# Moving the landmarks' softmax between the two halves of C v

## The chip, the cores and the metric

The kernel runs on one NeuronCore of a Trainium2 chip. The metric is the device time of one execution in microseconds (us). Every engine of the core works through its own queue of instructions in order: TensorE (PE, with its weight loads shown as PEld), VectorE (DVE), ScalarE (ACT), GpSimd (POOL), and SyncE (SP), which here only issues transfers. Engines meet through semaphores.

## The reference, cut to what matters

Three stages follow each other: a Nystrom attention over 8 batches with 8 heads, 576 positions and head dimension 64, a squared-ReLU layer pair over the 4608 tokens (512 to 2048 to 512), and a top-1 mixture of 8 experts. The change is in the attention:

```python
q_lm = q.reshape(B, H, m, S // m, D).mean(axis=3)      # m = 32 landmarks
k_lm = k.reshape(B, H, m, S // m, D).mean(axis=3)
A = sm(q, k_lm)        # sm: scaled scores, softmax over the last axis
Bm = sm(q_lm, k_lm)
C = sm(q_lm, k)
Z = Bm.transpose(0, 1, 3, 2) / (norm1(Bm) * norm_inf(Bm) + 1e-06)
for _ in range(6):
    Z = 2 * Z - Z @ Bm @ Z
out = A @ Z @ C @ v
```

`Bm` is the landmarks' own softmax, 32 by 32 for each head. `C v` is 32 by 64 for each head. Both must be there before the iteration for `Z` starts.

## The kernel before

For each batch the attention is a "unit" of small steps (`unit`). Heads go in two groups of four (`hg` 0 and 1), with four heads times 32 landmarks on the 128 partitions. Batch 0's unit runs in a prologue of its own, with `u["early"]` set and with high priority. The units of batches 1 to 7 are side work: they are generated one step at a time, by `point`, while the main work of an earlier batch runs. The main work is `gemm`, with `second`: each batch in two halves of 288 columns, each half in 16 pieces of 6 matmuls into `hp` (line 998) and 12 into `acc` (line 1048). A rate for each half (`RATES`) says how many side steps come with each point. `weave` takes two lists of steps in turn. So the order in which instructions are written down is set by these rates and weaves; a scheduler at build time then orders each engine's queue by that order and by what its model holds to be ready, and gives out buffers.

What the change touches is in these functions:

- `scores_c` makes the scores of C for one head group and one half of the columns, copies them to `ec` (ACT), takes the maximum (DVE, line 497), and after the second half makes the exponential with the row sum in `mc[..., 3]` (ACT, line 504).
- `softmax_b` is the landmarks' own softmax, three steps: 16 small matmuls into a bank (line 346, input `lm`), maximum and exponential (lines 523 to 528), then a chain of small DVE instructions (lines 533 to 560) to the norms, and `diagonal` (line 647), which lays `Bm` out as the weights `dg` of the iteration. Two of its instructions, lines 557 and 560, have nothing to do with `Bm`: they turn the row sum of C into its reciprocal, `mc[..., 5]`.
- `transposed_c(u, j)`, j = 0, 1, 2, transposes four blocks of `ec` on PE (line 349, input `ec`) and copies them to `et` on ACT (line 572).
- `values(u, hg)` multiplies `et` by `v` for one head group on PE (line 346, inputs `v,et`, 24 products that show as 48 matmuls). It scales the result into `bc` on DVE (line 587). At its end it issues a load of `v`: `values(u, 0)` issues the three transfers of this batch's second half, `values(u, 1)` those of the next batch's first half (`load_v`, line 371, on SP). Each half has one buffer, so a load waits for the product that last read the buffer.
- `inverse` is the iteration (line 346, inputs `bc,dg` and then `eu,dg`).

PSUM banks of the side work come from one pool of three (`aux`, through `bank()`), which the main work also uses for the gate's logits and routing. `values(u, 0)` takes a bank for both halves of C v (`u["pc"]`) and it is free again when `values(u, 1)` has been scaled. During batch 1's unit (and until about 141 us) the first layer's weights of the second matmul are still being converted (`convert`: lines 153 to 167 and 191 on ACT, DVE and POOL).

Of the kernel before, what the change touches and what calls it, by code (L numbers as in the profile page):

```python
# [9 lines left out]
F32 = mybir.dt.float32  # L10
# [4 lines left out]
ALU = mybir.AluOpType  # L15
# [4 lines left out]
B, H, S, D = 8, 8, 576, 64  # L20
LM = 32
# [62 lines left out]
class Kernel:  # L84
# [395 lines left out]
    def scores_c(self, u, hg, c):  # L480

        nc = self.nc
        if hg == c == 0:
            u["mc"] = self.sm.tile([128, 2, 8], F32, tag="mc", name="mc")
            u["ec"] = self.wk.tile([128, 2, S], F32, tag="ec", name="ec")
        sc = self.bank()
        for h in range(4):
            p, x = self.columns(u, "k", hg, h, c)
            self.matmul(sc[32 * h:32 * h + 32, 0:HC], lhsT=u["ql"][p, hg, h, :], rhs=x, start=True, stop=True)
        to, src = u["ec"][:, hg], sc[:, 0:HC]  # L490
        if u["pe"]:
            to = to.rearrange("p (r c i l) -> p c i r l", c=2, i=3, l=LM)[:, c]
            src = src.rearrange("p (i r l) -> p i r l", i=3, l=LM)
        else:
            to = to[:, c * HC:(c + 1) * HC]
        nc.scalar.copy(out=to, in_=src)
        nc.vector.tensor_reduce(out=u["mc"][:, hg, c:c + 1], in_=sc[:, 0:HC], axis=AX.X, op=ALU.max)
        if c == 1:

            mc, ec = u["mc"][:, hg], u["ec"][:, hg]  # L500
            nc.vector.tensor_scalar(
                out=mc[:, 2:3], in0=mc[:, 0:1], scalar1=mc[:, 1:2], scalar2=-SCALE / SEG, op0=ALU.max, op1=ALU.mult
            )
            nc.scalar.activation(
                out=ec, in_=ec, func=ACTF.Exp, bias=mc[:, 2:3], scale=SCALE / SEG, accum_out=mc[:, 3:4]
            )

    def softmax_b(self, u):

        nc, sm = self.nc, self.sm  # L510
        wide = [128, 2, LM]
        pb = self.bank()
        for hg in range(2):
            for h in range(4):
                self.matmul(
                    pb[32 * h:32 * h + 32, 32 * hg:32 * hg + 32],
                    lhsT=u["ql"][0:64, hg, h, :], rhs=u["kl"][0:64, hg, h, :], start=True, stop=True,
                )
        pb = pb[:, 0:2 * LM].rearrange("p (g l) -> p g l", g=2)
        bc = u["bc"] = sm.tile([128, 2, LM + D], F32, tag="bc", name="bc")  # L520
        mb = u["mb"] = sm.tile([128, 2, 12], F32, tag="mb", name="mb")
        bm = bc[:, :, 0:LM]
        nc.vector.tensor_reduce(out=mb[:, :, 0], in_=pb, axis=AX.X, op=ALU.max)
        nc.vector.tensor_scalar(
            out=mb[:, :, 1], in0=mb[:, :, 0], scalar1=-SCALE / SEG / SEG, scalar2=None, op0=ALU.mult
        )
        for hg in range(2):
            nc.scalar.activation(
                out=bc[:, hg, 0:LM], in_=pb[:, hg], func=ACTF.Exp, bias=mb[:, hg, 1:2], scale=SCALE / SEG / SEG,
                accum_out=mb[:, hg, 2:3],  # L530
            )
        yield STEP
        nc.vector.tensor_scalar(out=mb[:, :, 2], in0=mb[:, :, 2], scalar1=1e-9, scalar2=None, op0=ALU.add)
        nc.vector.reciprocal(out=mb[:, :, 3], in_=mb[:, :, 2])
        nc.vector.tensor_tensor(out=bm, in0=bm, in1=mb[:, :, 3].unsqueeze(2).to_broadcast(wide), op=ALU.mult)
        bt = sm.tile([128, 3, 2, LM], F32, tag="bt", name="bt", bufs=1)
        for hg in range(2):
            nc.vector.transpose(out=bt[:, 0, hg], in_=bc[:, hg, 0:LM])
        nc.vector.tensor_reduce(out=mb[:, :, 4], in_=bm, axis=AX.X, op=ALU.add)
        nc.vector.tensor_reduce(out=mb[:, :, 5], in_=bt[:, 0], axis=AX.X, op=ALU.add)  # L540
        yield STEP
        nc.vector.tensor_copy(
            out=bt[:, 1:3].rearrange("p a g l -> p g a l"),
            in_=mb[:, :, 4:6].unsqueeze(3).to_broadcast([128, 2, 2, LM]),
        )
        bn = sm.tile([128, 2, 2, LM], F32, tag="qs", name="bn", bufs=1)
        nc.vector.transpose(
            out=bn.rearrange("p a g l -> p (a g l)"), in_=bt[:, 1:3].rearrange("p a g l -> p (a g l)")
        )
        nc.vector.tensor_reduce(  # L550
            out=mb[:, :, 6:8].rearrange("p g a -> p a g"), in_=bn, axis=AX.X, op=ALU.max
        )
        nc.vector.tensor_tensor(out=mb[:, :, 8], in0=mb[:, :, 6], in1=mb[:, :, 7], op=ALU.mult)
        nc.vector.tensor_scalar(out=mb[:, :, 8], in0=mb[:, :, 8], scalar1=1e-6, scalar2=None, op0=ALU.add)
        nc.vector.reciprocal(out=mb[:, :, 9], in_=mb[:, :, 8])
        nc.vector.tensor_scalar(out=mb[:, :, 10], in0=mb[:, :, 9], scalar1=-1.0, scalar2=None, op0=ALU.mult)
        nc.vector.tensor_scalar(
            out=u["mc"][:, :, 4], in0=u["mc"][:, :, 3], scalar1=1e-9, scalar2=None, op0=ALU.add
        )
        nc.vector.reciprocal(out=u["mc"][:, :, 5], in_=u["mc"][:, :, 4])  # L560
        self.diagonal(u, bc)
        yield STEP

# [10 lines left out]
    def values(self, u, hg):  # L574

        if hg == 0:
            u["pc"] = self.bank()
        b = u["b"]
        for r in range(R6):
            for h in range(4):  # L580
                self.matmul(
                    u["pc"][32 * h:32 * h + 32, hg * D:(hg + 1) * D],
                    lhsT=u["et"][:, R6 * hg + r, 32 * h:32 * h + 32],
                    rhs=self.vt[b, hg][:, h, r * D:(r + 1) * D],
                    start=(r == 0), stop=(r == R6 - 1),
                )
        self.nc.vector.tensor_scalar(
            out=u["bc"][:, hg, LM:], in0=u["pc"][:, hg * D:(hg + 1) * D], scalar1=u["mc"][:, hg, 5:6], scalar2=None,
            op0=ALU.mult,
        )  # L590
        if (b, 1) not in self.vt:
            self.load_v(b, 1)
        elif hg == 1:
            self.load_v(b + 1, 0)
# [84 lines left out]
    def unit(self, u):  # L679
# [23 lines left out]
                yield STEP  # L703

        def cv():
            yield from self.softmax_b(u)
            for j in range(2):
                self.transposed_c(u, j)
                yield STEP
            self.values(u, 0)  # L710
            yield STEP
            self.transposed_c(u, 2)
            yield STEP

# [29 lines left out]
        if u["early"]:  # L744
            yield from weave(self.sooner(itertools.chain(cv(), zcv())), itertools.chain(tq(), a()))
        else:
            yield from weave(cv(), tq())
            yield from weave(zcv(), a())
# [749 lines left out]
```

## Time and profile before

| | |
|---|---|
| Time, median of 3 runs | 1337.75 us (1334.39 to 1339.83) |
| Profiled execution | 1340.34 us, of which its span is 1338.5 us |
| PE busy | 1275.7 us, 95% |
| DVE busy | 781.5 us, 58% |
| ACT busy | 633.6 us, 47% |
| POOL busy | 384.5 us, 29% |
| Mean granted TensorE clock | 0.977 of full speed |

Busy times are of one profiled execution, the only one with a trace. The page cuts the span into 40 slices of 33.5 us; a digit is the busy share of a slice in tenths. A busy PE is not PE at its peak: the ends of matmuls are modelled. An engine's idle time is put down to the last event that released it.

### The profile page before, as it was taken

How to read it: one execution, taken by the hardware profiler on the slowest of the kernel's cores; microseconds unless marked ns; L12 is line 12 of the kernel's file. 1: busy time of each engine (PE TensorE's matmuls, PEld its weight loads, DVE VectorE, ACT ScalarE, POOL GpSimd, SP SyncE). 2: the span in 40 equal slices, each digit the busy share in tenths (PEclk: the TensorE clock that was granted, in tenths of full speed). 3: DMA queues.
4: the chain of work that ended last, by engine and by line, in shares of the span. 5: the costliest groups of instructions: out<-in, count | busy, mean ns of one | idle time of the engine just before them, and what ended most of it. 6: DMA issues, size and time to landing. Idle time of an engine off the chain costs nothing.

```text
span 1338.5 us, 25101 instructions
## 1 busy us (share of the span) xinstructions
PE 1275.7 (95%) x9458; PEld 1114.2 (83%) x9458; DVE 781.5 (58%) x1743; ACT 633.6 (47%) x1402; POOL 384.5 (29%) x311
## 2 busy tenths in 40 slices
PE   6587999999999999999999999999999999999997
PEld 4276868688788888898989999998888888888886
DVE  7999868768769897687653433454423233233231
ACT  5596454445535557545654344344334334334331
POOL 3566112113013034313622112024323323233120
PEclk7588999999999999999999999999999999999999
DMA  9866283462623247613652112014344354342321
GB/s 324 273 222 192 86 269 85 173 199 89 217 70 112 72 127 211 172 63 95 206 146 67 43 35 67 1 48 146 99 130 139 100 156 120 109 150 92 116 93 38
DMA packets 126587, 172.38 MB, mean 129 GB/s; under 512 B 10558, under 2 KB 84062, under 8 KB 126462
## 3 DMA queue, kind: packets, MB, share of 16 engines
q1 hardware_dynamic: 126030, 170.11, 41.6%
q8 instruction: 76, 1.25, 0.4%
q0 software_dynamic: 288, 0.43, 0.1%
q14 instruction: 49, 0.40, 0.1%
q10 hardware_dynamic: 144, 0.20, 0.0%
HBM read 128.19 MB, written 42.51 MB: 128 GB/s over the span
## 4 chain that ended last, share of the span: by engine, by line
PE 74%; DVE 11%; DMA 7%; ACT 3%; issue 2%; POOL 1%; SPq 1%; POOLq 0%; DVEq 0%; ACTq 0%
PE acc L1048 24%; PE hp L1238 15%; PE y L1274 13%; PE hp L998 11%; PE bank L346 6%; PE y L1286 2%; DMA raw<-in_moe_w_in_dram 2%; DVE sums L382 2%; DVE gl L1015 2%; DMA g<-gs 2%; DVE g L1011 1%; PE pl L1075 1%; DVE m L164 1%; DMA w<-win 1%; DMA t<-in_q_dram 1%
## 5 line engine op out<-in xcount | busy, mean ns | idle before, releaser
L1048 PE MATMUL acc<-gh,wo 128*128 128x288 f32 x2048 | 459.2, 300 | 1.6 <-POOL wo L191 0.7
L1048 PEld LDWEIGHTS acc<-gh,wo 128*128 128x128 f32 x2048 | 344.1, 190 | 27.1 <-issue 18.2
L1048 PE MATMUL acc<-gl,wo 128*128 128x288 f32 x1024 | 290.3, 301 | 10.2 <-DVE gl L1015 9.7
L998 PE MATMUL hp<-ab,gb 128*128 128x288 f32 x1536 | 254.8, 301 | 0.9 <-ACT r L1009 0.5
L998 PEld LDWEIGHTS hp<-ab,gb 128*128 128x128 f32 x1536 | 217.7, 189 | 19.6 <-issue 6.9
L1011 DVE TENSOR_TENSOR g<-r 128x288 f32<-128x288 f32 x239 | 130.3, 546 | 162.5 <-ACT r L1009 161.7
L1009 ACT ACTIVATE r<-hp 128x288 f32<-128x288 f32 x256 | 105.8, 413 | 245.1 <-PE hp L998 240.6
L1238 PEld LDWEIGHTS hp<-xs,s 128*128 128x128 f32 x1536 | 210.7, 188 | 9.0 <-issue 0.9
L1238 PE MATMUL hp<-xs,s 128*128 128x288 f32 x1536 | 215.5, 295 | 0.0
L1048 PEld LDWEIGHTS acc<-gl,wo 128*128 128x128 f32 x1024 | 194.6, 190 | 22.8 <-DVE gl L1015 17.5
L1274 PE MATMUL y<-s,h 128*128 128x512 f32 x768 | 190.3, 395 | 0.0
L1274 PEld LDWEIGHTS y<-s,h 128*128 128x128 f32 x768 | 141.0, 188 | 29.4
L1015 DVE TENSOR_TENSOR gl<-g,gh 128x288 fp32r<-128x288 f32 x256 | 143.2, 560 | 26.8 <-ACT gh L1014 8.9
L191 POOL TENSOR_TENSOR s<-r,s 128x512 fp32r<-128x512 f32 x64 | 83.1, 1299 | 245.6 <-ACT s L188 245.6
L191 DVE TENSOR_TENSOR s<-r,s 128x512 fp32r<-128x512 f32 x64 | 53.1, 830 | 154.4 <-ACT s L188 154.4
L191 POOL TENSOR_TENSOR gb<-gr,gb 128x512 fp32r<-128x512 f32 x56 | 74.5, 1331 | 226.6 <-ACT gb L188 143.6
L188 ACT CAST s<-r 128x512 fp32r<-128x512 f32 x128 | 78.2, 616 | 118.8 <-PE y L1286 92.6
L1247 DVE SCALAR_TENSOR_TENSOR h<-hp,h 128x64 fp32r<-128x64 f32 (+2 forms) x192 | 62.6, 354 | 109.5 <-ACT h L1244 109.5
L1014 ACT ACTIVATE gh<-r 128x288 fp32r<-128x288 f32 x256 | 114.4, 447 | 6.4
L1244 ACT ACTIVATE h<-hp 128x288 fp32r<-128x288 f32 x128 | 52.6, 411 | 132.1 <-PE hp L1238 118.2
L382 DVE TENSOR_REDUCE sums<-t 128x32 f32<-128x576 f32 x64 | 71.2, 1165 | 9.3 <-DMA t<-in_q_dram 5.8
L191 POOL TENSOR_TENSOR xs<-xr,xs 128x1152 fp32r<-128x1152 f32 x16 | 45.7, 2860 | 68.3 <-ACT xs L188 63.2
(195 smaller groups left out, 1350.8 us busy)
## 6 DMA issues: line engine op xcount, KB each, us to landing
r<-in_moe_w_dram SPq DMA_DIRECT2D x128, 256.0 KB
w<-win SPq DMA_DIRECT2D x80, 256.0 KB
gr<-g SPq DMA_DIRECT2D x56, 256.0 KB
t<-in_k_dram SPq DMA_DIRECT2D x16, 576.0 KB
t<-in_q_dram SPq DMA_DIRECT2D x16, 576.0 KB
v<-in_v_dram SPq DMA_DIRECT2D x48, 192.0 KB
x_d<-x SPq DMA_DIRECT2D x16, 576.0 KB
xr<-x_d SPq DMA_DIRECT2D x16, 576.0 KB
```

The source lines that it names most:

```text
L188: hi = self.nc.scalar.copy(out=t[:, 0], in_=raw)
L191: (lo_eng or self.nc.gpsimd).tensor_tensor(out=t[:, 1], in0=raw, in1=t[:, 0].bitcast(F32), op=ALU.subtract)
L346: self.last_pe = self.nc.tensor.matmul(out, **kw)
L382: self.nc.vector.tensor_reduce(out=s[:, 0, ds], in_=t[:, :, ds].rearrange("p s d -> p d s"), axis=AX.X, op=ALU.add)
L998: mm = nc.tensor.matmul(hp[:, 0:HC], lhsT=g[:, l, hg, fs], rhs=at[:, r, hg, :], start=(i == 0), stop=(i == 5))
L1009: nc.scalar.activation(out=r, in_=hp[:, 0:HC], func=ACTF.Relu, scale=1.0 / 256)
L1011: nc.vector.tensor_tensor(out=g2, in0=r, in1=r, op=ALU.mult)
L1014: nc.scalar.activation(out=gh, in_=r, func=ACTF.Square)
L1015: nc.vector.tensor_tensor(out=gl, in0=g2, in1=gh.bitcast(F32), op=ALU.subtract)
L1048: nc.tensor.matmul(acc[m][:, 0:HC], lhsT=self.wo[f][:, l, ms], rhs=r, start=(f == 0 and i == 0), stop=(f == NFC - 1 and i == 2),)
L1238: nc.tensor.matmul(hp[:, 0:HC], lhsT=s1[:, l, kk, :], rhs=xs[j, c][:, r, kk, :], start=(k == 0), stop=(k == 3 * KD - 1),)
L1274: mm = nc.tensor.matmul(acc[t], lhsT=l, rhs=s2[:, r, :], start=(first and k == 0), stop=(last and k == 2))
```

## The change

For batches with `u["early"]` unset, that is 1 to 7, the three steps of `softmax_b` are made after `values(u, 0)` and not ahead of `transposed_c(u, 0)`. So that `values(u, 0)` has what it needs, the two instructions for the reciprocal of C's row sum move to the end of `scores_c`, for batch 0 too, and the tile `bc`, which both write parts of, is made by whichever comes first.

```diff
@@ scores_c
+        if hg == c == 1:
+            mc = u["mc"]
+            nc.vector.tensor_scalar(out=mc[:, :, 4], in0=mc[:, :, 3], scalar1=1e-9, scalar2=None, op0=ALU.add)
+            nc.vector.reciprocal(out=mc[:, :, 5], in_=mc[:, :, 4])
+
+    def place_bc(self, u):
+        if "bc" not in u:
+            u["bc"] = self.sm.tile([128, 2, LM + D], F32, tag="bc", name="bc")
+        return u["bc"]
@@ softmax_b
-        bc = u["bc"] = sm.tile([128, 2, LM + D], F32, tag="bc", name="bc")
+        bc = self.place_bc(u)
...
-        nc.vector.tensor_scalar(
-            out=u["mc"][:, :, 4], in0=u["mc"][:, :, 3], scalar1=1e-9, scalar2=None, op0=ALU.add
-        )
-        nc.vector.reciprocal(out=u["mc"][:, :, 5], in_=u["mc"][:, :, 4])
@@ values
-            out=u["bc"][:, hg, LM:], in0=u["pc"][:, hg * D:(hg + 1) * D], scalar1=u["mc"][:, hg, 5:6], scalar2=None,
+            out=self.place_bc(u)[:, hg, LM:], in0=u["pc"][:, hg * D:(hg + 1) * D], scalar1=u["mc"][:, hg, 5:6], scalar2=None,
@@ unit
         def cv():
-            yield from self.softmax_b(u)
+
+            if u["early"]:
+                yield from self.softmax_b(u)
             for j in range(2):
                 self.transposed_c(u, j)
                 yield STEP
             self.values(u, 0)
             yield STEP
+            if not u["early"]:
+                yield from self.softmax_b(u)
             self.transposed_c(u, 2)
             yield STEP
```

## Rows read from the trace of the kernel before

**Rows 1.** The page, section 1, and PE in 40 slices.
```profile
PE 1275.7 (95%) x9458; PEld 1114.2 (83%) x9458; DVE 781.5 (58%) x1743; ACT 633.6 (47%) x1402; POOL 384.5 (29%) x311
...
PE   6587999999999999999999999999999999999997
```

**Rows 2.** Stretches: length, busy us (instructions) by engine, PE clock, DMA share, GB/s.
```profile
60.00:140.00 80.00, 66.82 (x538) 54.55 (x535) 75.01 (x125) 62.55 (x151) 48.91 (x37) 0.91 0.62 195
140.00:660.00 520.00, 506.87 (x4311) 433.65 (x4310) 405.25 (x921) 274.10 (x640) 136.71 (x127) 1.00 0.46 140
660.00:1330.00 670.00, 666.96 (x4261) 605.81 (x4259) 249.38 (x578) 264.46 (x545) 172.15 (x117) 1.00 0.33 97
```

**Rows 3.** Waits of PE from 60 us on: us in total, times, longest us.
```profile
PE acc L1048 <- DVE gl L1015: 9.7, 11, 2.8
PE bank L346 <- DMA v<-in_v_dram: 3.4, 2, 2.1
PE bank L346 <- ACT et L572: 1.6, 1, 1.6
...
PE bank L346 <- DVE bc L587: 1.0, 1, 1.0
...
PE bank L346 <- ACT gs L934: 0.8, 2, 0.6
```

**Rows 4.** PE in order of time, 100 to 130 us: start, us, line, operation.
```profile
109.57 1.51 PE L346 MATMUL bank<-v,et 96*32 96x64 f32 x48
...
117.11 0.43 PE L346 MATMUL bank<-v,et 96*32 96x64 f32 x16 [2.13 <-DMA v<-in_v_dram]
```

**Rows 5.** PE in order of time, 186 to 219 us (batch 2's unit).
```profile
195.91 0.43 PE L346 MATMUL bank<-v,et 96*32 96x64 f32 x16 [1.64 <-ACT et L572]
...
202.23 0.46 PE L346 MATMUL bank<-bc,dg 128*128 128x96 f32 x2 [1.04 <-DVE bc L587]
...
207.21 0.88 PE L346 MATMUL bank<-v,et 96*32 96x64 f32 x48 [1.30 <-DMA v<-in_v_dram]
...
213.12 0.58 PE L346 MATMUL bank<-eu,dg 128*128 128x96 f32 x4
...
218.07 0.58 PE L346 MATMUL bank<-eu,dg 128*128 128x96 f32 x4
```

**Rows 6.** SP's issues in order of time, 106 to 215 us.
```profile
111.14 1.28 SPq L371 DMA_DIRECT2D v<-in_v_dram  x3
...
197.03 1.86 SPq L371 DMA_DIRECT2D v<-in_v_dram  x3
```

**Rows 7.** Short stretches, columns as in rows 2.
```profile
118.75:122.15 3.40, 3.40 (x47) 2.95 (x49) 3.37 (x5) 2.75 (x6) 1.32 (x2) 0.50 0.00 0
197.25:200.65 3.40, 3.11 (x14) 2.77 (x13) 2.20 (x4) 1.14 (x3) 0.81 (x1) 0.50 1.03 317
```

**Rows 8.** DVE in order of time, 92 to 130 us.
```profile
111.15 0.28 DVE L587 TENSOR_SCALAR bc<-bank,mc 128x64 f32<-128x64 f32 x1 [0.22 <-PE bank L346]
...
118.42 2.28 DVE L382 TENSOR_REDUCE sums<-t 128x32 f32<-128x576 f32 x2 [0.91 <-DMA t<-in_q_dram]
```

**Rows 9.** Groups by line, DVE, 60 to 660 us: busy, mean ns, idle before.
```profile
L647 DVE TENSOR_TENSOR dg<-bc,h 128x256 f32<-128x256 f32 x7 | 4.0, 573 | 0.0
...
L523 DVE TENSOR_REDUCE mb<-bank 128x2 f32<-128x64 f32 x7 | 1.4, 203 | 0.0
```

**Rows 10.** DVE in order of time, 16 to 34 us (batch 0's unit).
```profile
23.90 0.17 DVE L557 TENSOR_SCALAR mc<-mc 128x2 f32<-128x2 f32 x1
...
28.24 0.24 DVE L587 TENSOR_SCALAR bc<-bank,mc 128x64 f32<-128x64 f32 x1
```

**Rows 11.** PE in order of time, 436 to 456 us (batch 5's unit).
```profile
437.99 0.29 PE L346 MATMUL bank<-lm 64*32 64x32 f32 x12
...
438.98 0.60 PE L349 MATMUL bank<-ident,ec 128*96 128x128 f32 x4
```

**Rows 12.** Waits of SP's queue, whole span.
```profile
SPq L371 <- PE bank L346: 32.1, 12, 7.9
```

## The prediction, made blind

> **What bounds the kernel now.** I read the page first, then stretches, then the waits of the engine that they point to, and then single instructions around the changed code. The page says that PE is busy for 95% of the span, and its row of slices is a line of nines after the first 130 us [rows 1]. The stretches say where the rest is: in 60 to 140 us PE is busy 66.82 of 80 us, and DVE 75.01 of 80, so that stretch is paced by DVE, which still converts weights there. From 140 to 660 us PE is idle for 520.00 - 506.87 = 13.1 us, from 660 to 1330 us for only 3.0 us [rows 2]. The units of batches 1 to 7 run between 60 and 660 us. So nearly everything that the change touches is side work beside an engine that is already full, and it counts only as far as PE stands still for it, or as far as a standstill lowers PE's clock.
>
> The waits of PE name the standstills [rows 3]. The largest, 9.7 us in 11, is main work: `acc` waits for `gl` from a late DVE. Next come 3.4 us in 2 for the load of `v`, 1.6 us for a copy of `et`, 1.0 us for `bc`. All of these touch the code that is moved, so the question is which of them the new order takes away and which it makes.
>
> **The two waits for v.** In batch 1, `values(u, 0)` starts at 109.57 us, takes 1.51, and `values(u, 1)` is held until 117.11 us with 2.13 us of idle before it [rows 4]. In batch 2 the first half's last products run at 195.91 us and the second half is held until 207.21, with 1.30 us idle [rows 5]. The loads are issued as soon as the first half has read the buffer: at 111.14 us and at 197.03 us [rows 6]. From the first issue to the end of the wait is 117.11 - 111.14 = 6.0 us and 207.21 - 197.03 = 10.2 us. The load cannot start before the product that empties its one buffer, so only a longer way from the first half to the second hides it.
>
> **What the change does to that way.** `cv` and `tq` are woven, one step of each in turn. Before, 4 steps lie between `values(u, 0)` and `values(u, 1)` in batches 2 to 7: a step of `tq`, `transposed_c(u, 2)`, two more of `tq`. After, the three steps of `softmax_b`, with three of `tq` between them, come on top: 10 steps. For batch 1, with fewer steps in `tq`, it is 2 and then 8. What a step lasts is read from the iteration, which is also woven one to one: 218.07 - 213.12 = 4.95 us for two steps, some 2.5 us each [rows 5]. Six more steps are an estimated 15 us. As the scheduler may pull side work together, I count on half of it, and 7 us still cover the 1.30 and the 2.13 us. So both waits go, in the order as written.
>
> **What they are worth.** In batch 2 PE is the bound, and the gain is the 1.30 us. For batch 1 the ends are further apart. After the wait of 2.13 us the granted clock is 0.50, or 1.2 GHz in place of 2.4, from 118.75 to 122.15 us, and PE is busy all 3.40 us of it [rows 7]; at full clock that work would take 1.70 us. So the upper end is 2.13 + 1.70 = 3.8 us. The lower end is set by DVE, which in this stretch has no time to give: around the wait it idles only 0.22 and 0.91 us [rows 8], 1.1 us in all. What PE wins above that, it would lose again at the next `gl`. I take 1.7 us, near the lower end, since DVE was the busier of the two [rows 2]. Together 3.0 us.
>
> The Trainium skill (DMA: Bandwidth & Descriptors, "Anatomy of one DMA") gives a transfer about 2.0 us plus its bytes over 436 GB/s, fitted on GpSimd's path. By that the 590 KB of one half would be there an estimated 3.4 us after the issue, no half would be waited for, and the change would hide nothing: 0 in place of 3.0 us. The 6.0 and 10.2 us of this trace [rows 4, 5, 6] differ from it, and go.
>
> **The moved steps themselves.** Nothing is added or dropped. For one batch `softmax_b` with `diagonal` is 16 small matmuls, 2 exponentials, and 19 DVE instructions between 203 ns (the first, line 523) and 573 ns (the last, line 647) [rows 9], by the means of the same view 4.8 us of DVE. They come later, by six steps. Who needs them next is `inverse(u, 0)`, and from the end of `softmax_b` to it there are still a step of `tq`, `transposed_c(u, 2)`, two of `tq`, `values(u, 1)` and one of scores: six steps, by the same 2.5 us some 15 us against 4.8 us of work. That cover is why I cost the move at nothing. Were it gone, `inverse` would wait as it does once for `bc`, 1.0 us [rows 3], in up to 7 batches: 0 to 7 us. The count of steps for a unit stays, so a unit ends where it did, and no batch's main work is held longer.
>
> The pair for the reciprocal (lines 557 and 560) goes from `softmax_b` to `scores_c`. In batch 0 it runs at 23.90 us, and its reader at 28.24 [rows 10]: over 4 us of room, so the prologue stays. In the others it could stand in DVE's queue and wait for the exponential; behind it would be the main work's `gl`. The scheduler put it after the exponential already; I cost it at 0, with 1 us for one late `gl` (9.7 / 11 is 0.9 us) [rows 3] as the upper end.
>
> Transfers: the three issues of `values(u, 0)` come earlier. SP stands before such an issue until PE has read the buffer, 32.1 us in 12, 2.7 us each [rows 12], and loads of `g` queue behind it. That stays as it is, only earlier; its longest, 7.9 us, was covered by loaded `g`, since no wait of PE names them [rows 3]. Cost 0.
>
> **Sum.** 1.30 + 1.7 = 3.0 us off. The profiled execution took 1340.34 us (span 1338.5 and 1.8 around it), which gives 1337.3; it lies 2.6 us above the median of the runs, so against the median the forecast is 1337.75 - 3.0 = 1334.8 us. About 0.5%, 6.7 us, is what a measurement of this kernel can tell from no change; this is less.
>
> **Rivals.**
>
> *More goes than the waits for v* (1328 us). In batch 2 the copies of `et` and of `bc` made PE wait 1.64 and 1.04 us [rows 5], the former followed by 197.25 to 200.65 us at clock 0.50 [rows 7]: another 1.7 us. If the new order takes these along with the full 3.8 us of batch 1, it is 1.30 + 3.8 + 1.64 + 1.04 + 1.7 = 9.5 us. For it: all lie in the moved stretch. Against it: DVE paces batch 1, and the `et` wait may only change places.
>
> *Nothing comes out* (1337.8 us). The scheduler may lay down nearly the same order, or the 1.30 us is eaten by one new wait. For it: in batch 5 the transposes of C run 1.0 us after the landmark products [rows 11], though the text puts two more steps of each list between them; so the executed order is not the written one.
>
> *Slower: C v loses its cover* (1345 us). `softmax_b` stood between the exponential of C and its transposes. Now `transposed_c` follows `scores_c` at once, and PE's queue is in order: if a transpose or a product reaches PE before the exponential or the copy of `et` is done, main work behind it waits too. The price by the one such wait is 1.64 us, and with a stretch at half clock 3.3 us. It shows as slower from (6.7 + 3.0) / 3.3, three batches of seven, on; at three it is 1334.8 + 9.9 = 1345. Against it: two woven steps still lie between the last scores and the blocks of the second head group, and the scheduler waits for what its model knows.
>
> *Slower: banks* (1342 us). The bank of C v is now held for 10 steps, and two of three are left for landmark products, transposes, the pieces of `g` and the gate. One wait of PE for a bank's reader (`gs`) is 0.4 us [rows 3], with half clock 2.1; in half of the batches 7 us. Against it: the pool is used little at a time by batches 3 to 5. The Trainium skill (Perfetto Trace Analysis, "Identifying the Most-Contended Engine" and what follows it) reads a gap that repeats on the saturated engine as a possible lack of PSUM; the trace before shows no such repeating gap.
>
> **Chances.** Forecast 0.48 (its own range 1331.5 to 1338), nothing comes out 0.14, more goes 0.24, lost cover 0.09, banks 0.05. Faster by over 0.5% is the case in which more goes, 0.24; slower the last two together, 0.14; within 0.5% the rest, 0.62. The range reaches to the cases on both sides, 1327 to 1344 us: it leaves out the far half of each.
>
> **What would show it.** In the profile after, PE's wait for `v` [rows 3] should be gone, with at least 10 us between the two halves of C v in each of batches 1 to 7; the landmark products should lie between these halves; PE idle in 140 to 660 us should be about 12 us. If the wait for `v` goes and the time stays, look for new waits of PE before `ident,ec` or `v,et` blocks (lost cover), for waits on `gs` or `x` (banks), or for a longer 60 to 140 us stretch paced by DVE. The prediction is wrong if the reordered queues lose `gl` in time more often than the 11 waits of before, which no row here can price for a new order.

## The result, and the profile after

The changed kernel takes 1350.74 us (median of 6 runs, 1346.34 to 1354.96) against 1337.83 us for the kernel before, also of 6: a ratio of 1.0098, 95% interval 1.0076 to 1.012. It is slower by 12.9 us. The profiled execution took 1351.13 us, its span is 1349.4 us.

The page of the changed kernel answers to [rows 1]:

```profile
span 1349.4 us, 25106 instructions
...
PE 1284.1 (95%) x9458; PEld 1116.3 (83%) x9458; DVE 789.1 (58%) x1743; ACT 635.1 (47%) x1402; POOL 382.7 (28%) x311
...
PE   6588999999999999999999999999999999999997
```

The same 9458 matmuls are there, and PE is busy 1284.1 - 1275.7 = 8.4 us longer. So most of the loss shows as busy time and not as idle time. The waits of PE from 60 us on, which answer to [rows 3], do not show it either:

```profile
PE acc L1057 <- DVE gl L1024: 9.9, 12, 2.7
PE bank L346 <- DMA v<-in_v_dram: 4.8, 4, 3.0
PE hp L1007 <- ACT r L1018: 2.8, 3, 1.8
PE bank L349 <- POOL sums L385: 2.5, 2, 1.6
```

The wait for `v`, which was to go, has grown from 3.4 us in 2 to 4.8 us in 4: batch 1's is gone, batch 2's is longer, and small ones in batches 3, 6 and 7 are new. To see where the time went I followed the main work: it is the same 256 pieces in both kernels, so the time at which ACT makes `gh` for the k-th piece can be compared. At the start of batch 1's second half the changed kernel is 1.1 us behind (265.2 against 264.1 us), in batch 5's second half 10.8 us (734.7 against 723.9). From there on the distance stays. So I took that stretch of equal work as one window in each kernel (columns as in [rows 2]). The kernel before:

```profile
264.10:723.90 459.80, 450.45 (x3817) 396.10 (x3816) 343.69 (x789) 247.33 (x574) 133.21 (x117) 1.00 0.44 133
```

The changed kernel:

```profile
265.20:734.70 469.50, 458.60 (x3817) 398.94 (x3816) 350.45 (x789) 248.79 (x574) 132.57 (x117) 1.00 0.43 130
```

With 3817 matmuls in both, the window is 9.7 us longer. PE's idle time is 459.80 - 450.45 = 9.3 us before and 10.9 after, 1.6 us more. The other 8.2 us, from 450.45 to 458.60, are busy time. The Trainium skill (Perfetto Trace Analysis, "Identifying the Most-Contended Engine") warns that the busy share of matmuls is no measure of how near PE is to its peak, because matmuls are pipelined; this pair of rows agrees.

One execution of each says little on a few us, but four runs below help. In e1 PE has the very order of before, in e11 and e15 it has it from 264 us on, and in e12 it has the order of the changed kernel (the instruction lists of the traces are equal). The same window in e1, then in e12:

```profile
263.60:720.40 456.80, 449.43 (x3817) 396.10 (x3816) 341.79 (x788) 247.75 (x573) 133.94 (x117) 1.00 0.44 134
262.80:730.40 467.60, 456.88 (x3817) 397.64 (x3816) 349.06 (x788) 248.79 (x573) 132.87 (x117) 1.00 0.43 131
```

So more busy time belongs to the new order. In the mean of four executions of the old order and two of the new, the window is 10.9 us longer: 7.2 us of busy time at full clock, 2.9 us of idle time, and 0.9 us of clock.

Two things make PE busier with the same work. One is the clock. In the changed kernel PE waits 1.60 us for the sums of batch 5's unit, and then stands at clock 0.50 (1.2 GHz). PE in order of time, 425 to 436 us, and a short stretch behind it:

```profile
428.07 0.33 PE L349 MATMUL bank<-ident,sums 128*128 128x128 f32 x1 [1.60 <-POOL sums L385]
```
```profile
429.35:432.70 3.35, 3.35 (x14) 3.35 (x15) 3.19 (x5) 0.73 (x2) 1.71 (x2) 0.50 0.64 212
```

PE is busy throughout, so half of it, 1.7 us, is lost. That leaves 8.2 - 1.7 = 6.5 us. This stretch is chance and not the order: e12 has the same wait of 1.60 us at the same place and no half clock after it.

```profile
425.39 0.33 PE L349 MATMUL bank<-ident,sums 128*128 128x128 f32 x1 [1.60 <-POOL sums L385]
```

The other is how the side work lies in PE's queue, C v first of all. Batch 3's unit in the kernel before, PE in order of time, the products of C v alone:

```profile
282.23 0.42 PE L346 MATMUL bank<-v,et 96*32 96x64 f32 x14
...
283.56 0.75 PE L346 MATMUL bank<-v,et 96*32 96x64 f32 x34
...
289.65 0.31 PE L346 MATMUL bank<-v,et 96*32 96x64 f32 x4
...
290.87 0.86 PE L346 MATMUL bank<-v,et 96*32 96x64 f32 x44
```

and in the changed kernel, with what stands behind the third piece:

```profile
278.74 0.65 PE L346 MATMUL bank<-v,et 96*32 96x64 f32 x32
...
280.31 0.42 PE L346 MATMUL bank<-v,et 96*32 96x64 f32 x12
...
281.64 0.31 PE L346 MATMUL bank<-v,et 96*32 96x64 f32 x4
281.88 0.40 PE L1057 MATMUL acc<-gh,wo 128*128 128x288 f32 x1
282.12 0.29 PE L1057 MATMUL acc<-gl,wo 128*128 128x288 f32 x1
282.25 0.43 PE L1057 MATMUL acc<-gh,wo 128*128 128x288 f32 x2
...
288.22 0.31 PE L346 MATMUL bank<-v,et 96*32 96x64 f32 x4 [0.41 <-DMA v<-in_v_dram]
...
289.71 0.32 PE L346 MATMUL bank<-v,et 96*32 96x64 f32 x8
290.69 0.54 PE L346 MATMUL bank<-v,et 96*32 96x64 f32 x24
292.15 0.42 PE L346 MATMUL bank<-v,et 96*32 96x64 f32 x12
```

The 96 matmuls come in 4 pieces before and in 7 after, with main work between. A piece has a price of its own. The four products at 281.64 us and the main matmul behind them take until 282.12, 0.48 us. A main matmul in a row takes 0.13 us (282.12 to 282.25), and four products in a long piece 4 x 0.65 / 32 = 0.08 us. So the side piece and the way out of it cost some 0.27 us more than their work, all of it shown as busy. The way in has a price too. Over the window, in both kernels, a main matmul takes 0.22 us (median, from start to start) ahead of a product whose weights have 32 or 64 columns (the second number in `96*32`), and 0.13 us ahead of one with 128, such as a transpose. That makes some 0.36 us for a visit to C v. PE's queue holds C v in 30 pieces before and in 43 after, 6 of them batch 0's in both.

C v is not alone in this, and at 0.36 us its pieces do not make up the 6.5 us: in the window they are 19 before and 28 after, 3.2 us. The scores against the landmarks (`x,lm`, weights `64*32`) are torn as well. First a group in the kernel before, then one of the changed kernel, with four main matmuls between its two pieces:

```profile
289.03 0.69 PE L346 MATMUL bank<-x,lm 64*32 64x288 f32 x8
```
```profile
293.97 0.67 PE L346 MATMUL bank<-x,lm 64*32 64x288 f32 x2
...
295.30 0.68 PE L346 MATMUL bank<-x,lm 64*32 64x288 f32 x6
```

Two products last nearly as long as eight, so this tear costs some 0.6 us. I call "visits" the times when PE comes from a product with 128 weight columns to one with fewer, whichever it is. In the window they are 88 before and 97 after.

### The profile page after: what moved, and what is told of

Read it like the earlier page. It is cut to its first block, busy times and chain, and to the rows that moved or that the text cites. A ratio compares the mean times of both kernels' runs of the same rounds, so it can differ in the third digit from the quotient of the medians.

```text
span 1349.4 us, 25106 instructions
## 1 busy us (share of the span) xinstructions
PE 1284.1 (95%) x9458; PEld 1116.3 (83%) x9458; DVE 789.1 (58%) x1743; ACT 635.1 (47%) x1402; POOL 382.7 (28%) x311
## 4 chain that ended last, share of the span: by engine, by line
PE 77%; DVE 12%; DMA 5%; ACT 3%; issue 2%; POOL 1%; SPq 1%; DVEq 0%; POOLq 0%; ACTq 0%
PE acc L1057 24%; PE hp L1247 15%; PE y L1283 13%; PE hp L1007 12%; PE bank L346 7%; DVE sums L382 2%; DMA g<-gs 2%; PE y L1295 2%; DVE gl L1024 2%; DVE g L1020 1%; DVE x L413 1%; DMA v<-in_v_dram 1%; PE pl L1084 1%; PE bank L349 1%; DVE m L164 1%
## 5 line engine op out<-in xcount | busy, mean ns | idle before, releaser
L1024 DVE TENSOR_TENSOR gl<-g,gh 128x288 fp32r<-128x288 f32 x256 | 146.3, 572 | 21.5 <-ACT gh L1023 4.2
```

The costliest lines, as they stand in the source:

```text
L1024: nc.vector.tensor_tensor(out=gl, in0=g2, in1=gh.bitcast(F32), op=ALU.subtract)
```

## The experiments

Each was timed against the kernel before on the same chip, in 4 to 12 runs; the kernel before had medians of 1336.6 to 1338.2 us there. "Pieces" are those of C v in PE's queue, with 6 of batch 0. "Visits", to products with fewer than 128 weight columns, are counted in the window of equal work. "PE busy" is of the window of equal work, less half of any stretch at clock 0.50 in it.

| | Ratio to before, 95% interval | Median us | Pieces | Visits | PE busy, us | PE idle, us |
|---|---|---|---|---|---|---|
| before | | 1337.8 | 30 | 88 | 450.4 | 9.3 |
| changed | 1.0098 (1.0076 to 1.0120) | 1350.7 | 43 | 97 | 456.9 | 10.9 |
| e1, pair alone | 1.0000 (0.9989 to 1.0012) | 1336.7 | 30 | 88 | 449.4 | 7.4 |
| e2, between | 1.0059 (1.0046 to 1.0072) | 1344.6 | 33 | 95 | 455.2 | 11.2 |
| e3, changed, two banks | 1.0125 (1.0108 to 1.0142) | 1352.1 | 39 | 94 | 455.3 | 11.3 |
| e4, before, two banks | 1.0042 (1.0029 to 1.0055) | 1343.1 | 33 | 92 | 452.3 | 9.2 |
| e5, before, rate 0.66 | 1.0056 (1.0034 to 1.0078) | 1344.7 | 35 | 97 | 453.7 | 10.2 |
| e6, changed, rate 0.66 | 1.0093 (1.0070 to 1.0116) | 1350.5 | 45 | 102 | 457.8 | 9.9 |
| e7, before, swapped | 1.0083 (1.0060 to 1.0105) | 1348.8 | 36 | 95 | 454.2 | 9.7 |
| e8, changed, swapped | 1.0098 (1.0073 to 1.0123) | 1350.6 | 41 | 96 | 454.5 | 10.8 |
| e9, changed, last first | 1.0061 (1.0038 to 1.0083) | 1345.7 | 26 | 89 | 450.6 | 12.5 |
| e10, before, last first | 1.0018 (1.0005 to 1.0030) | 1339.7 | 27 | 89 | 450.5 | 10.5 |
| e11, batches 1 and 2 | 1.0002 (0.9990 to 1.0014) | 1337.6 | 34 | 88 | 449.1 | 7.0 |
| e12, batches 3 to 7 | 1.0096 (1.0072 to 1.0121) | 1348.6 | 39 | 97 | 456.9 | 10.7 |
| e13, e9 and two banks | 1.0069 (1.0051 to 1.0086) | 1346.8 | 27 | 90 | 450.4 | 12.2 |
| e14, e9 without batch 6 | 1.0048 (1.0031 to 1.0066) | 1343.2 | 28 | 89 | 450.6 | 9.8 |
| e15, between, batch 1 | 0.9966 (0.9953 to 0.9979) | 1332.7 | 31 | 88 | 449.8 | 8.1 |
| e16, before, torn | 1.0022 (1.0010 to 1.0034) | 1339.7 | 40 | 93 | 452.9 | 7.0 |

Busy and idle are of one execution each. Before and e1 have the same order of PE and still differ by 1.0 and 1.9 us, so only larger steps count there. Beside these, the visits order the busy time well: with 88 to 90 it is 449.1 to 450.6 us, with 92 to 96 it is 452.3 to 455.3, with 97 to 102 it is 453.7 to 457.8. The pieces of C v alone do not: e2 has 33, as e4 has, and is 2.9 us busier.

### First four: the pair, the cover, the bank

**e1** keeps the softmax first and moves only the pair:

```diff
         def cv():
-            if u["early"]:
-                yield from self.softmax_b(u)
+            yield from self.softmax_b(u)
...
-            if not u["early"]:
-                yield from self.softmax_b(u)
```

> Only the reciprocal pair moves to scores_c; the landmarks' softmax stays first. PE's queue is then the same as before. Theory H (the bank of C v is held across the landmarks' softmax, so two of three banks are left) and theory C (the transposes of C lose their cover) both expect the time of before, 1337.8 us, within 3 us. If the pair is the cause (DVE stands for the exponential), 1345 us or more.

Measured 1.0000 (0.9989 to 1.0012). The pair costs nothing that can be seen.

**e2** puts the softmax between the transposes and C v:

```diff
             for j in range(2):
                 self.transposed_c(u, j)
                 yield STEP
+            if not u["early"]:
+                yield from self.softmax_b(u)
             self.values(u, 0)
             yield STEP
-            if not u["early"]:
-                yield from self.softmax_b(u)
```

> The landmarks' softmax is made after the two transposes but ahead of the first half of C v: the transposes lose their cover as in the changed kernel, the bank of C v is held as shortly as before. Theory C: as slow as the changed kernel, 1346 to 1355 us. Theory H: the time of before, 1334 to 1341 us. A third theory, R (any new order misses what the scheduler's model expected, at places that have nothing to do with the moved step): anywhere between 1334 and 1355 us.

1344.6 us lies 1.4 us under theory C's range and 3.6 above theory H's: neither the cover of the transposes nor the bank alone. Theory R's range holds both others, so this run could not speak against it.

**e3** and **e4** give the second half of C v a bank of its own, in the changed kernel and in the one before:

```diff
-        if hg == 0:
+        if hg == 0 or not u["early"]:
             u["pc"] = self.bank()
```

> The changed kernel, but the second half of C v takes a bank of its own in batches 1 to 7, so that no bank is held across the landmarks' softmax. Theory H: back to 1336 to 1342 us. Theory C: stays at 1346 us or more. Theory R: it moves by several us in either way.

> The kernel before with the second half of C v in a bank of its own: the control for the two banks. Theory H: equal to before or up to 2 us faster, 1335 to 1339 us, since the bank was held for a short way. Theory R: it can come out several us off, and then a few us of the difference between the kernels say nothing on the moved step.

e3 is no faster than the changed kernel, so theory H falls as the cause of the loss. e4 is the surprise: an edit that takes nothing away costs the kernel before 0.42%. A few us of difference may belong to any new order of the queues.

### Second four: new orders with the softmax left in its place

**e5** and **e6** set `RATE = 0.66` in place of 0.65 in both kernels. **e7** and **e8** swap the lists, which puts every step of C v one step later:

```diff
-            yield from weave(cv(), tq())
+            yield from weave(tq(), cv())
```

> The kernel before with RATE 0.66 in place of 0.65: no step is moved, but from the third batch of the main work on side steps come a little sooner, which makes a new order of the queues. Theory R (the order of before happens to fit the chip, and any new order loses some us): 1340 to 1350 us. Theory M (the moved step itself costs, by splitting C v into more visits of PE): 1337 us, within 3 us.

> The changed kernel with RATE 0.66. Theory R: anywhere between 1340 and 1355 us, and no further from the run with the same rate and the old order than 3 us. Theory M: some 10 us above the run with the same rate and the old order.

> The kernel before with the two lists of steps woven the other way round (the q side first, then C v), in batches 1 to 7: every step of C v comes one step later, nothing else. Theory R: 1340 to 1350 us. Theory M: 1337 us, within 3 us.

> The changed kernel with the same swap of the two lists. Theory R: within 3 us of the run before it. Theory M: some 10 us above it.

Both theories are half right. New orders of the kernel before cost 0.42% (e4), 0.56% (e5) and 0.83% (e7) with the softmax not moved: theory R. The changed kernel beside its partner of the same edit is 9.1 us (two banks), 5.8 us (rate) and 1.8 us (swap, within the noise) slower; theory M had expected some 10, theory R at most 3. Its orders hold 39 to 45 pieces, those of before 30 to 36. The new orders of the kernel before are no clean control for busy time, since they pay it too: e4, e5 and e7 have 92, 97 and 95 visits where before has 88.

### Third four: the pieces, and which batches

**e9** and **e10** let the first product of a half need the block copied last:

```diff
-        for r in range(R6):
+        rs = range(R6) if u["early"] else range(R6 - 1, -1, -1)
+        for r in rs:
...
-                    start=(r == 0), stop=(r == R6 - 1),
+                    start=(r == rs[0]), stop=(r == rs[-1]),
```

> The changed kernel, but in batches 1 to 7 each half of C v takes its six blocks in reverse order, so that its first product needs the block that is copied last, and the rest can follow without a break. In PE's queue C v then stands in 26 pieces; it is 43 in the changed kernel and 30 in the one before. Theory M (C v torn into more visits of PE, each with an entry, an exit and a chance to wait): 1338 to 1344 us. Theory R (any new order loses): 1343 to 1351 us, whatever the pieces.

> The kernel before with the same reverse order: C v in 27 pieces in place of 30. Theory M: 1334 to 1339 us. Theory R: 1342 to 1349 us, as with the other new orders of the kernel before.

e9 gives back 1350.7 - 1345.7 = 5 us (its interval and that of the changed kernel just overlap), and it does so where theory M says. The window of equal work in e9:

```profile
265.80:730.70 464.90, 452.36 (x3818) 397.04 (x3817) 346.57 (x789) 248.52 (x574) 131.97 (x117) 1.00 0.43 132
```

Less 1.7 us at half clock, PE's busy time is 450.6 us, that of the kernel before. The whole 6.5 us are gone. There are 8 visits fewer than in the changed kernel; not all of this is C v, since `x,lm` is torn in one group in place of three. But the time is not gone: 1345.7 us is 1.7 us outside theory M's range and inside theory R's. e10, 1339.7 us, is 0.7 us outside M's and 2.3 under R's.

**e11** and **e12** make the change for some batches alone, by `u["b"] in (1, 2)` and `u["b"] > 2` in place of `not u["early"]`:

> The change for batches 1 and 2 alone, where the two waits for v were (34 pieces of C v). By the prediction's sum 1334.8 us. Theory M: 1338 to 1341 us. Theory R: 1342 to 1349 us.

> The change for batches 3 to 7 alone (39 pieces of C v). Theory M: most of the loss, 1345 to 1351 us. Theory R: 1342 to 1349 us, and the two parts of the change do not add up to the whole.

1.0002 and 1.0096: within the noise the parts add up to the whole, against theory R, and all of it comes from batches 3 to 7, where the kernel before had no wait for `v` to lose. e11 has 34 pieces and no loss, 0.4 us under theory M's range and 2.8 above the prediction's sum; its busy time in the window, which begins behind the units of batches 1 and 2, is that of before.

### Last four: what is left, and a check from the other side

In e9's trace the largest wait of PE in that window is for a bank, in batch 6's unit, where pieces of `g` use the three banks too. PE in order of time:

```profile
543.10 0.85 PE L346 MATMUL bank<-wi,wt 128*128 128x512 f32 x3
...
550.44 1.65 PE L346 MATMUL bank<-wi,wt 128*128 128x512 f32 x3 [3.31 <-ACT gs L944]
```

**e13** is e9 with e3's edit, **e14** is e9 with the old place of the softmax in batch 6 (`u["b"] in (1, 2, 3, 4, 5, 7)`):

> The changed kernel with the reverse order of blocks, and with a bank of its own for the second half of C v. With the reverse order alone 8.4 us of loss are left; in its trace the largest wait of PE is 3.31 us for a bank in batch 6's unit, where pieces of g use the same three banks. If holding the bank of C v makes that wait (theory H, for that place alone): 1338 to 1342 us. If not (theory R): 1343 to 1351 us.

> The changed kernel with the reverse order, but in batch 6, the one whose unit runs beside the doubled pieces of g, the landmarks' softmax stays first. Theory H for that place: 1338 to 1342 us. Theory R: 1343 to 1351 us.

In e13 the wait for `gs` shrinks to 0.3 us, and the time stays at 1346.8: other waits and stretches at half clock (10 us of them in the window, in an execution that was the slowest of 6) come in its place. e14 is at 1343.2 us, 0.3% to 0.7% above before, 1.2 us over theory H's range and inside R's; its interval overlaps e9's. The wait goes with either edit, but it is not shown that the held bank makes it: the changed kernel holds its bank across the softmax too and has no wait for `gs` in the window (e12, with the same order, has one of 0.8 us), and in e9 the copy `gs` came late because ACT had stood 2.15 and 0.87 us for loads of `gr`. Nor is it shown to be the rest of the loss.

**e16** tears C v in the kernel before, with the softmax left first:

```diff
             for j in range(2):
+                if j == 1 and not u["early"]:
+                    self.values(u, 0, range(0, 2))
                 self.transposed_c(u, j)
                 yield STEP
-            self.values(u, 0)
+            if not u["early"]:
+                self.values(u, 0, range(2, 4))
+                self.values(u, 0, range(4, 6))
+            else:
+                self.values(u, 0)
```

`values` gets the blocks to take, and scales and loads at the last one only.

> The kernel before with the first half of C v written down in parts, two blocks of the six ahead of the second transpose step, so that C v stands in 40 pieces in PE's queue in place of 30; the landmarks' softmax stays first and no step is added. Theory M: ten more pieces at the 0.3 us by which the reverse order paid for each, 1340 to 1344 us. If the pieces cost nothing: 1337 us, within 2 us.

1.0022 (1.0010 to 1.0034): 3 us for 10 pieces, 0.3 us a piece, slightly under the range that I gave. The time alone proves little, as e10 lost 2.4 us with 3 pieces fewer. But its PE busy time is 452.92 - 450.45 = 2.5 us above that of the kernel before, for 7 more pieces in a window with as many matmuls, and e10's is not above it at all:

```profile
263.40:723.30 459.90, 452.92 (x3817) 396.75 (x3816) 348.89 (x788) 248.12 (x573) 132.34 (x117) 1.00 0.43 133
```

**e15** makes the softmax between the transposes and C v in batch 1 alone:

```diff
-            if u["early"]:
+            if u["b"] != 1:
                 yield from self.softmax_b(u)
             for j in range(2):
                 self.transposed_c(u, j)
                 yield STEP
+            if u["b"] == 1:
+                yield from self.softmax_b(u)
             self.values(u, 0)
             yield STEP
-            if not u["early"]:
-                yield from self.softmax_b(u)
```

> The landmarks' softmax between the transposes and C v in batch 1 alone, the old order in the others. The run with it so in all batches was 5 us ahead of the kernel before at 141 us and lost that and more from batch 5's unit on. If the lead belongs to batch 1's order and nothing gives it back: 1333 us, faster than both kernels. If it was chance or is given back: 1337 to 1342 us.

1332.7 us, 0.9966 (0.9953 to 0.9979): faster than both kernels. Its stretch from 60 to 140 us, which stands beside the first of [rows 2]:

```profile
60.00:140.00 80.00, 65.62 (x553) 51.65 (x550) 73.77 (x128) 63.90 (x153) 48.85 (x38) 0.98 0.60 198
```

The granted clock is 0.98 where it was 0.91, and DVE is busy 73.77 us in place of 75.01. After e4 to e8 I read it as an order that happens to fit that stretch better, which is not shown; that it would survive another edit elsewhere was not tried.

## Why the prediction was wrong

**The bound** was read rightly: main work on PE sets the pace, and the side work counts only where PE pays for it. But "as far as PE stands still for it, or as far as a standstill lowers PE's clock" leaves out what PE pays while it is busy. It put that at nothing. Of the 9.7 us in the window of equal work, 6.5 us are of that kind; in the mean of the executions with equal orders it is 7.2 of 10.9.

**The step that failed** is "What the change does to that way": six more steps between the halves of C v, an estimated 15 us, of which half would cover the loads. The way hardly grew. In batch 2 of the changed kernel, PE in order of time and SP's issues:

```profile
195.49 0.43 PE L346 MATMUL bank<-v,et 96*32 96x64 f32 x16 [0.46 <-ACT et L577]
...
206.62 0.88 PE L346 MATMUL bank<-v,et 96*32 96x64 f32 x48 [3.00 <-DMA v<-in_v_dram]
```
```profile
197.28 2.52 SPq L371 DMA_DIRECT2D v<-in_v_dram  x3
```

From the last piece of the first half to the second half it is 206.62 - 195.49 = 11.1 us; it was 207.21 - 195.91 = 11.3 us [rows 5]. The wait did not go but grew from 1.30 to 3.00 us, and a stretch of 3.4 us at clock 0.50 follows it. In batch 3 the second half starts 6.6 us after the last piece of the first (281.64 to 288.22) and waits 0.41 us for `v`. Over the seven batches this distance changed by -0.3 to +2.2 us, where 7 to 15 had been forecast; the 10 us that the prediction asked for in each batch are there in batch 2 alone. So written steps do not set the distance. That the scheduler lets PE come to the second half when its model holds the load to be there would fit, but no run tests it. In batch 2 the load's own time sets it, 9.3 us (197.28 to 206.62) after 10.2 before. The Trainium skill's figure (DMA: Bandwidth & Descriptors, "Anatomy of one DMA"), an estimated 3.4 us, is far under both.

**The gain in batches 1 and 2** of 3.0 us: e11 measures -1.3 to +1.9 us by its interval. Batch 1's wait of 2.13 us did go, as forecast; PE starts the second half after 0.44 us:

```profile
116.57 0.42 PE L346 MATMUL bank<-v,et 96*32 96x64 f32 x14 [0.44 <-issue]
```

It gave back next to nothing, as the bound by DVE had it, and less than the 1.7 us taken: from 60 to 205 us PE waits 7.1 us in 6 for `gl` where it waited 4.8 in 3. Batch 2's 1.30 us did not come. It was no property of the order: e1, with the same order of PE, has no wait for `v` in batch 2. The prediction had one execution to read it from.

**The pair, the moved softmax, SP's wait at no cost**: right for the pair (e1). No run shows SP's wait by itself. The cover of the softmax held: in the full list of the changed kernel's waits of PE, of which the first four lines stand above, `inverse` has no wait for `bc`, where it had 1.0 us before. Late `gl` did not multiply over the whole run either: 12 waits in place of 11. PE's idle time from 140 to 660 us, which was to be about 12 us, is 15.4.

**The rivals.** "Lost cover" named the right place in part and the wrong price. The transposes and the first half of C v now stand close behind the exponential, and the scheduler fills in main work between blocks that are copied one after the other: that is my reading of the order. It costs as visits and not as waits. e9 takes pieces away and with them the busy time; e16 adds them and pays in busy time. Why `x,lm` is torn as well is not shown. "Banks" falls for the whole (e3), and at one place (e9, batch 6) it is possible.

**What stays open.** Of the 12.9 us some 7 are busy time of more visits, by the traces; e9, which has hardly more visits than before, gave back 5 us. The rest is not tied to a step. The kernel before itself loses 6 to 11 us with new orders (e4, e5, e7): in the window 1.8 to 3.7 us of it is busy time again, and at most 1 us is idle time. And few visits are not enough: e9, e13 and e14 have 89 or 90 and still lose 7 to 10 us. The traces of e9 and e13 show waits and half-clock stretches at places far from the moved step. Why most new orders wait more than that of before is argued only: the rates of the side work may fit that one order.

## What to carry to other kernels

Where side work is woven into an engine that is already full, count how often the engine is sent to it and back, and not only what it waits for: the price, 0.36 us for C v and some 0.6 us for `x,lm` here, stands in no list of waits and shows as busy time with as many instructions. It shows when two kernels are compared over the same work. Products over blocks that become ready one by one can be begun with the last block, if they are torn: that gave 5 us back in the changed kernel (e9) and cost the kernel before 2.4 us (e10). A wait in a single trace may not be there in the next execution of the same order. Before a change of 1% is put down to its mechanism, move something neutral and see what that alone costs; here it was 0.4% to 0.8%.

## What the runs showed of the hardware

A main matmul took 0.22 us from start to start ahead of a product with 32 or 64 weight columns, and 0.13 us ahead of one with 128. Two products of `x,lm` in a piece of their own took 0.67 us, eight in a row 0.69.

A wait of 1 to 3 us of PE was followed by a stretch at clock 0.50 in some executions and not in others. In the changed kernel the 1.60 us at 428 us were, and 1.7 us were lost; in e12 the same wait in the same order, at 425 us, was not. In the kernel before neither the 1.30 us at 207 us nor any other wait of PE after 201 us was. So a wait of that length can cost twice itself or only itself, and the order does not tell which.
